# Feed-forward matmuls that read their moving columns as two interleaved halves

## The chip, the cores and the metric

The kernel runs on one core of a Trainium2 chip. The metric is device time in microseconds (us), the median of several runs of the same program.

## What is computed

Eight sequences of 3008 tokens with 256 features go through a spectral layer (a real Fourier transform along the sequence, a complex 256x256 product with a bias, a soft threshold, the inverse transform) and then, token by token, through a feed-forward layer:

```python
def _moe_ref(x, w_in, w_out):
    h = x @ w_in              # 24064 x 256 by 256 x 2048
    g = h * np.cos(h)
    return (g @ w_out).astype(np.float32)   # 2048 x 256
```

## The kernel before

**The spectral layer** is done by stages of small matmuls that the program calls `stage_a`, `stage_b` and `stage_c` (with special versions for the first sequences). The last of them, `stage_c`, leaves the tokens of a sequence with the features on the partitions, as a pair of float32r tiles `xTh` and `xTl` (a high part and the rest), for a tile of 512 tokens at a time: two chunks `c` of 128 features, each with 512 tokens side by side (lines 723 to 725). A sequence has six such tiles, five of 512 tokens and a last one of 448.

**The feed-forward layer** runs over sequences `b`, token tiles `t` and 16 chunks `f` of 128 hidden features. A step (`moe_step`, lines 765 to 790) has six matmuls into a PSUM tile `ph`, with the weights as the stationary operand and the tokens as the moving one: for each of the two feature chunks the high weights by `xTh` (line 772), the high weights by `xTl` (line 773) and the low weights by `xTh` (line 774). The cosine follows on ScalarE and VectorE (lines 779 to 783), then a split of the result into `gh` (ScalarE, line 784) and `gl` (VectorE or GpSimd, lines 785, 148 and 151). Three steps later (`SKEW`) `second` takes the pair up, with six more matmuls into two PSUM tiles `po`, the moving operand being `gh` (lines 742 and 743) and `gl` (line 748; line 745 in the very last step):

```python
mm(h, win[:, 0, c, fs], th[:, c, :n], start=c == 0, stop=False)
...
mm(po[e][:, :n], wo[0][:, 0, f, es], gh[:, :n], start=f == first, stop=False)
```

Here `n` is 512 or 448, and each of these operands is a run of `n` consecutive float32r words on each of 128 partitions. That is 8 x 6 x 16 = 768 steps of 12 matmuls, 9216 in all.

**The order.** While one sequence is in the feed-forward layer, the spectral stages of the next two are woven between its steps: `pull` in `moe_step` takes pieces of them by a budget of written costs (lines 866 to 875), so the order on TensorE is fixed when the program is built. The first stages, before the first feed-forward step, are written out by hand.

**Other matmuls that the prediction uses.** Line 323 multiplies plain float32 tiles of 96x512 (not float32r), line 520 plain float32 tiles of 128x256. **Other reads that it uses.** Line 299 copies a PSUM tile `p` of 128x512 to SBUF in another order, in turn on ScalarE and VectorE:

```python
(nc.vector.tensor_copy if n % 2 else nc.scalar.copy)(
    dst[:, :, :, 2 * n:2 * n + 2], p.rearrange("p (j c m) -> p c m j", j=2, c=2)[:, :, :96])
```

With `j` innermost it reads word 0, word 256, word 1, word 257 and so on. Line 201 reads every second word of an SBUF tile. Lines 724, 762, 783 and 784 read runs of consecutive words.

**The host** puts the result's columns, which come out by tile, back in the order of the sequence (line 919).

Of the kernel before, what the change touches and what calls it, by code (L numbers as in the profile page):

```python
# [19 lines left out]
NB, N, D, FF = 8, 3008, 256, 2048  # L20
# [7 lines left out]
NTT = 6  # L28
# [29 lines left out]
def _index():  # L58
    n1, n2 = np.arange(64), np.arange(48)
    return (47 * n1[:, None] + 64 * n2[None, :]) % N  # L60


def _constants():
# [50 lines left out]
def tile_body(ctx: ExitStack, tc, x, x2, w_r, w_i, b_r, b_i, w_in, w_out,  # L114
# [27 lines left out]
    win = cp.tile([128, 2, 2, FF], F32R, name="win")  # L142
    wo = [cp.tile([128, 2, NFC, 256], F32R, name="wout")]

    mm = nc.tensor.matmul
# [87 lines left out]
    raws, mark = [], {}  # L233
# [493 lines left out]
            yield 0.49  # L727


    pend = []  # L730
    outs, part = {}, {}

    def second(b, t, f, gh, gl):
        n = 512 if t < NTT - 1 else 448
        first, last_f = next((lo, hi - 1) for v, lo, hi in phases(b) if v == t and lo <= f < hi)
        if f == first:
            outs[0] = [ps.tile([128, 512], F32, tag=f"o{e}", name=f"po{e}", bufs=1) for e in range(2)]
        po = outs[0]
        end = (b, t, f) == (NB - 1, NTT - 1, NFC - 1)
        for e in range(2):  # L740
            es = slice(128 * e, 128 * e + 128)
            mm(po[e][:, :n], wo[0][:, 0, f, es], gh[:, :n], start=f == first, stop=False)  # L742
            mm(po[e][:, :n], wo[0][:, 1, f, es], gh[:, :n], start=False, stop=False)  # L743
            if end:
                mm(po[e][:, :n], wo[0][:, 0, f, es], gl[:, :n], start=False, stop=True)
        for e in range(0 if end else 2):
            es = slice(128 * e, 128 * e + 128)
            mm(po[e][:, :n], wo[0][:, 0, f, es], gl[:, :n], start=False, stop=f == last_f)  # L748
        if f != last_f:
            return  # L750
        for e in range(2):
            if last_f < NFC - 1:
                part[t, e] = wk.tile([128, 512], F32, tag=("yh", "yl", "z")[t], name="part", bufs=2)
                nc.scalar.copy(part[t, e], po[e])  # L754
                continue
            if e == 0:
                outs[1] = pool["mo"].tile([128, 2, 512], F32, tag="ob", name="ob", bufs=1)
            ob = outs[1][:, e]
            if first:
                nc.vector.tensor_tensor(out=ob, in0=po[e], in1=part.pop((t, e)), op=ALU.add)  # L760
            else:
                (nc.vector.tensor_copy if end and e else nc.scalar.copy)(ob[:, :n], po[e][:, :n])
            nc.sync.dma_start(out[b, e, :, 512 * t:512 * t + n], ob[:, :n])

    def moe_step(b, t, f, pull):
        th, tl = xT[b, t]
        n = 512 if t < NTT - 1 else 448
        ph = ps.tile([128, 512], F32, tag="h", name="ph", bufs=3)
        h = ph[:, :n]
        fs = slice(128 * f, 128 * f + 128)  # L770
        for c in range(2):
            mm(h, win[:, 0, c, fs], th[:, c, :n], start=c == 0, stop=False)  # L772
            mm(h, win[:, 0, c, fs], tl[:, c, :n], start=False, stop=False)  # L773
            mark["ph"] = mm(h, win[:, 1, c, fs], th[:, c, :n], start=False, stop=c == 1)  # L774
        u = pool["mo"].tile([128, 512], F32, tag="u", name="u", bufs=4)
        k = u.bitcast(I32)
        gh = pool["mo"].tile([128, 512], F32R, tag="gh", name="gh", bufs=SKEW + 1)
        gl = pool["mo"].tile([128, 512], F32R, tag="gl", name="gl", bufs=SKEW + 1)
        nc.scalar.activation(k[:, :n], h, AF.Identity, bias=0.25, scale=1.0 / TWO_PI)  # L779
        nc.vector.scalar_tensor_tensor(out=u[:, :n], in0=h, scalar=1.0 / TWO_PI, in1=k[:, :n],  # L780
                                       op0=ALU.mult, op1=ALU.subtract)
        nc.scalar.activation(u[:, :n], u[:, :n], AF.Sin, bias=HALF_PI, scale=TWO_PI)  # L782
        nc.vector.tensor_tensor(out=u[:, :n], in0=h, in1=u[:, :n], op=ALU.mult)  # L783
        mark["gh"] = nc.scalar.copy(gh[:, :n], u[:, :n])  # L784
        (rest_pool if b == 0 and t < 3 and f < 8 or f % 4 in POOL_GL else rest)(gl[:, :n], u[:, :n], gh[:, :n])
        pend.append((b, t, f, gh, gl))
        pull()
        if len(pend) > SKEW:
            second(*pend.pop(0))
        pull()  # L790
# [3 lines left out]
    with tc.manual_schedule(), ExitStack() as first:  # L794
# [4 lines left out]
        p = ps.tile([128, 512], F32, tag="o0", name="pz", bufs=1)  # L799
# [17 lines left out]
    def phases(b):  # L817
        if b == 0:
            return [(t, f, f + 8) for f in (0, 8) for t in range(3)] + [(t, 0, NFC) for t in range(3, NTT)]
        return [(t, 0, NFC) for t in range(NTT)]  # L820
# [38 lines left out]
    for b in range(NB):  # L859
        fa = ahead(b)  # L860
        for i, (t, lo, hi) in enumerate(phases(b)):
            budget = [0.0]
            open_ = [True]
            cost = share(b, i) + C_COST * (len(c_next(b, i)) if i < len(phases(b)) - 1 else 1)
            hold = C_FROM if b == i == 0 else 0
            rate = cost / (hi - lo - 1 - hold) / 2

            def pull():
                budget[0] += rate
                while open_[0] and budget[0] > 0:  # L870
                    c = next(fa, None)
                    if c is None:
                        open_[0] = False
                    else:
                        budget[0] -= c

            for f in range(lo, hi):
                if b == 0 and i < FIRST_B:
                    if i or f >= W_FROM:
                        due += W_RATE  # L880
                    while due >= 1.0:
                        due -= 1.0
                        next(mw, None)
                moe_step(b, t, f, pull if f >= hold else lambda: None)
            while open_[0]:
                c = next(fa, None)
                if c is None:
                    open_[0] = False
            if hi == NFC:
                del xT[b, t]  # L890
    for p in pend:
        second(*p)
# [28 lines left out]
```

## Time and profile before

| what | us |
|---|---|
| median of 3 runs | 2629.59 (2629.4 to 2632.5) |
| the profiled execution, its own time | 2629.45 |
| its span, from the first to the last instruction | 2627.7 |

In the rows further down, PE is TensorE's matmuls, PEld its weight loads, DVE VectorE, ACT ScalarE, POOL GpSimd; L742 is line 742. A row of a group gives the line, the engine, the operation, the names of what is written and read with their shapes and a count, then the busy time of the group, the mean duration of one in ns, and idle time ahead of it. Matmuls overlap, and the profile models their ends, so the mean of one is not what it costs in a row of many: for that the difference of two starts is read from the timeline.

### The profile page before, as it was taken

The numbers are of one execution on the slowest core, as the hardware profiler recorded it, in microseconds if no ns is written. First come the engines' busy times: TensorE is split into PE (matmuls) and PEld (weight loads), VectorE is DVE, ScalarE is ACT, GpSimd is POOL, SyncE is SP. The second block draws the span as 40 slices with busy tenths as digits, with TensorE's granted clock in tenths as the row PEclk, the third lists the DMA queues.
The fourth block names the chain that finished last, engine by engine and source line by source line (L and its number), as shares of the span: only waits on it lengthen the run. The fifth ranks groups of instructions, "written<-read, shape, count | busy, mean of one in ns | idle before, by whom it ended". The sixth has DMA issues, their size and how long they took to land.

```text
span 2627.7 us, 38433 instructions
## 1 busy us (share of the span) xinstructions
PE 2618.9 (100%) x13180; PEld 2241.8 (85%) x13180; DVE 1917.8 (73%) x3237; ACT 1877.2 (71%) x3557; POOL 1085.3 (41%) x916
## 2 busy tenths in 40 slices
PE   9999999999999999999999999999999999999999
PEld 8788888888888888888888888888888888888888
DVE  6888876877667776777767777677776666766665
ACT  5787766777677776777767777677776666666666
POOL 5774543544334443344423444244442333322222
PEclk9999999999999999999999999999999999999999
DMA  7533312322123222233212232123221111010000
GB/s 208 177 97 98 105 61 77 94 87 90 55 60 93 86 85 59 60 93 98 75 56 62 91 96 75 55 62 103 89 71 53 47 53 43 25 54 22 9 17 16
DMA packets 126373, 194.26 MB, mean 74 GB/s; under 512 B 14131, under 2 KB 63619, under 8 KB 126177
## 3 DMA queue, kind: packets, MB, share of 16 engines
q1 hardware_dynamic: 120160, 171.94, 21.5%
q0 software_dynamic: 6016, 19.86, 2.4%
q8 instruction: 104, 1.70, 0.3%
q14 instruction: 93, 0.75, 0.1%
HBM read 119.92 MB, written 71.83 MB: 73 GB/s over the span
## 4 chain that ended last, share of the span: by engine, by line
PE 99%; DMA 0%; DVE 0%; SPq 0%; issue 0%; ACT 0%; ACTq 0%
PE ph L772 13%; PE po L742 13%; PE po L743 13%; PE ph L773 13%; PE po L748 13%; PE ph L774 13%; PE pc L715 4%; PE pb L396 3%; PE p L422 2%; PE p L421 2%; PE p L420 2%; PE pi L460 2%; PE pa L364 2%; PE p L520 1%; PE pa L323 1%; PE pa L297 0%
## 5 line engine op out<-in xcount | busy, mean ns | idle before, releaser
L148 POOL TENSOR_TENSOR gl<-u,gh 128x512 fp32r<-128x512 f32 (+1 forms) x396 | 507.8, 1283 | 958.0 <-ACT gh L784 754.9
L783 DVE TENSOR_TENSOR u<-ph,u 128x512 f32<-128x512 f32 (+1 forms) x768 | 520.5, 678 | 275.6 <-ACT u L782 258.5
L780 DVE SCALAR_TENSOR_TENSOR u<-ph,u 128x512 f32<-128x512 f32 (+1 forms) x768 | 518.9, 676 | 252.0 <-ACT u L779 242.4
L779 ACT ACTIVATE u<-ph 128x512 int32<-128x512 f32 (+1 forms) x768 | 450.1, 587 | 253.0 <-PE ph L774 241.2
L782 ACT ACTIVATE u<-u 128x512 f32<-128x512 f32 (+1 forms) x768 | 479.5, 625 | 202.1 <-DVE u L780 199.1
L772 PE MATMUL ph<-xTh,win 128*128 128x512 f32 (+1 forms) x1536 | 611.5, 398 | 1.4 <-DVE u L783 1.1
L742 PE MATMUL po<-gh,wout 128*128 128x512 f32 (+1 forms) x1536 | 598.7, 390 | 0.0
L774 PE MATMUL ph<-xTh,win 128*128 128x512 f32 (+1 forms) x1536 | 595.1, 387 | 0.0
L773 PE MATMUL ph<-xTl,win 128*128 128x512 f32 (+1 forms) x1536 | 595.1, 387 | 0.0
L743 PE MATMUL po<-gh,wout 128*128 128x512 f32 (+1 forms) x1536 | 594.8, 387 | 0.0
L784 ACT CAST gh<-u 128x512 fp32r<-128x512 f32 (+1 forms) x768 | 467.2, 609 | 137.1 <-DVE u L783 134.9
L748 PE MATMUL po<-gl,wout 128*128 128x512 f32 (+1 forms) x1534 | 477.0, 388 | 0.0
L774 PEld LDWEIGHTS ph<-xTh,win 128*128 128x128 f32 x1536 | 288.8, 188 | 54.4
L742 PEld LDWEIGHTS po<-gh,wout 128*128 128x128 f32 x1536 | 289.0, 188 | 51.7 <-ACT part L754 0.3
L743 PEld LDWEIGHTS po<-gh,wout 128*128 128x128 f32 x1536 | 289.0, 188 | 51.6
L772 PEld LDWEIGHTS ph<-xTh,win 128*128 128x128 f32 x1536 | 289.1, 188 | 49.6 <-DVE u L783 2.0
L748 PEld LDWEIGHTS po<-gl,wout 128*128 128x128 f32 x1534 | 285.6, 188 | 51.9
L773 PEld LDWEIGHTS ph<-xTl,win 128*128 128x128 f32 x1536 | 289.5, 188 | 46.0
L151 DVE TENSOR_TENSOR gl<-u,gh 128x512 fp32r<-128x512 f32 (+1 forms) x372 | 274.2, 737 | 49.8 <-ACT gh L784 42.2
L148 POOL TENSOR_TENSOR xh<-xt,xh 48x512 fp32r<-48x512 f32 x144 | 188.5, 1310 | 205.9 <-ACT xh L352 179.4
L446 POOL TENSOR_TENSOR z<-z,cl 128x512 f32<-128x512 f32 x84 | 110.0, 1309 | 208.4 <-DVE cl L445 197.6
L367 DVE TENSOR_TENSOR ao<-pa,ao 48x512 f32<-48x512 f32 x192 | 133.0, 693 | 22.2 <-ACT ao L366 17.1
(122 smaller groups left out, 3108.1 us busy)
## 6 DMA issues: line engine op xcount, KB each, us to landing
xt<-in_dram SPq DMA_DIRECT2D x192, 224.0 KB, 2.7
scr<-bo SPq DMA_DIRECT2D x95, 256.0 KB, 2.0
bt<-scr SPq DMA_DIRECT2D x96, 240.0 KB, 3.2
at<-scr SPq DMA_DIRECT2D x84, 256.0 KB, 2.7
out_dram<-ob SPq DMA_DIRECT2D x80, 256.0 KB, 2.2
scr<-ao SPq DMA_DIRECT2D x192, 96.0 KB, 1.9
fb<-in_dram POOLq DMA_DIRECT2D x46, 256.0 KB, 3.3
raw<-in_dram POOLq DMA_DIRECT2D x14, 512.0 KB, 4.3
```

Source lines behind the costliest of these rows:

```text
L148: return nc.gpsimd.tensor_tensor(out=lo, in0=x, in1=hi.bitcast(F32), op=ALU.subtract)
L742: mm(po[e][:, :n], wo[0][:, 0, f, es], gh[:, :n], start=f == first, stop=False)
L743: mm(po[e][:, :n], wo[0][:, 1, f, es], gh[:, :n], start=False, stop=False)
L748: mm(po[e][:, :n], wo[0][:, 0, f, es], gl[:, :n], start=False, stop=f == last_f)
L772: mm(h, win[:, 0, c, fs], th[:, c, :n], start=c == 0, stop=False)
L773: mm(h, win[:, 0, c, fs], tl[:, c, :n], start=False, stop=False)
L774: mark["ph"] = mm(h, win[:, 1, c, fs], th[:, c, :n], start=False, stop=c == 1)
L779: nc.scalar.activation(k[:, :n], h, AF.Identity, bias=0.25, scale=1.0 / TWO_PI)
L780: nc.vector.scalar_tensor_tensor(out=u[:, :n], in0=h, scalar=1.0 / TWO_PI, in1=k[:, :n], op0=ALU.mult, op1=ALU.subtract)
L782: nc.scalar.activation(u[:, :n], u[:, :n], AF.Sin, bias=HALF_PI, scale=TWO_PI)
L783: nc.vector.tensor_tensor(out=u[:, :n], in0=h, in1=u[:, :n], op=ALU.mult)
L784: mark["gh"] = nc.scalar.copy(gh[:, :n], u[:, :n])
```

## The change

All 9216 feed-forward matmuls take their moving operand through a new helper, `woven`, which orders the `n` columns as column 0, column n/2, column 1, column n/2 + 1 and so on; in words of the partition, 0, 256, 1, 257 for `n` = 512, and 0, 224, 1, 225 for 448. The stationary operand and the output are as before: the results are written side by side, in the order in which the columns are read. So `ph` holds the tokens in an order that is woven once, `po` in one that is woven twice, and the host undoes it with `_order`. No instruction is added or taken away, and no engine but TensorE is given another operand.

```diff
+def _order():
+    at = []
+    for t in range(NTT):
+        n = min(512, N - 512 * t)
+        w = np.arange(n).reshape(2, n // 2).T.reshape(-1)
+        at.append(512 * t + w[w])
+    return np.concatenate(at)
...
+    def woven(v):
+        return v.rearrange("p (b a) -> p a b", b=2)
+
...
-            mm(po[e][:, :n], wo[0][:, 0, f, es], gh[:, :n], start=f == first, stop=False)
-            mm(po[e][:, :n], wo[0][:, 1, f, es], gh[:, :n], start=False, stop=False)
+            mm(po[e][:, :n], wo[0][:, 0, f, es], woven(gh[:, :n]), start=f == first, stop=False)
+            mm(po[e][:, :n], wo[0][:, 1, f, es], woven(gh[:, :n]), start=False, stop=False)
...
-            mm(po[e][:, :n], wo[0][:, 0, f, es], gl[:, :n], start=False, stop=f == last_f)
+            mm(po[e][:, :n], wo[0][:, 0, f, es], woven(gl[:, :n]), start=False, stop=f == last_f)
...
-            mm(h, win[:, 0, c, fs], th[:, c, :n], start=c == 0, stop=False)
-            mm(h, win[:, 0, c, fs], tl[:, c, :n], start=False, stop=False)
-            mark["ph"] = mm(h, win[:, 1, c, fs], th[:, c, :n], start=False, stop=c == 1)
+            mm(h, win[:, 0, c, fs], woven(th[:, c, :n]), start=c == 0, stop=False)
+            mm(h, win[:, 0, c, fs], woven(tl[:, c, :n]), start=False, stop=False)
+            mark["ph"] = mm(h, win[:, 1, c, fs], woven(th[:, c, :n]), start=False, stop=c == 1)
...
-    res[:, idx[:, :47].reshape(2, 32, 47).transpose(1, 0, 2).reshape(-1)] = got
+    res[:, idx[:, :47].reshape(2, 32, 47).transpose(1, 0, 2).reshape(-1)[_order()]] = got
```

## Rows read from the trace of the kernel before

**Rows 1.** Page: busy us of each engine, then granted TensorE clock in 40 slices.
```profile
PE 2618.9 (100%) x13180; PEld 2241.8 (85%) x13180; DVE 1917.8 (73%) x3237; ACT 1877.2 (71%) x3557; POOL 1085.3 (41%) x916
...
PEclk9999999999999999999999999999999999999999
```
**Rows 2.** Page: the chain that ended last, shares by engine and by line.
```profile
PE 99%; DMA 0%; DVE 0%; SPq 0%; issue 0%; ACT 0%; ACTq 0%
PE ph L772 13%; PE po L742 13%; PE po L743 13%; PE ph L773 13%; PE po L748 13%; PE ph L774 13%; PE pc L715 4%; PE pb L396 3%; PE p L422 2%; PE p L421 2%; PE p L420 2%; PE pi L460 2%; PE pa L364 2%; PE p L520 1%; PE pa L323 1%; PE pa L297 0%
```
**Rows 3.** Groups by shape on PE: some of the feed-forward lines.
```profile
L772 PE MATMUL ph<-xTh,win 128*128 128x512 f32 x1280 | 513.4, 402 | 1.4 <-DVE u L783 1.1 <-ACT xTh L724 0.3
...
L742 PE MATMUL po<-gh,wout 128*128 128x512 f32 x1280 | 504.4, 394 | 0.0
...
L742 PE MATMUL po<-gh,wout 128*128 128x448 f32 x256 | 94.3, 368 | 0.0
...
L748 PE MATMUL po<-gl,wout 128*128 128x448 f32 x254 | 73.0, 367 | 0.0
...
L745 PE MATMUL po<-gl,wout 128*128 128x448 f32 x2 | 0.6, 366 | 0.0
```
**Rows 4.** Timeline, a step of 512 columns: start us, us, engine, line.
```profile
2559.85 0.39 PE L742 MATMUL po<-gh,wout 128*128 128x512 f32 x1
...
2560.08 0.19 PEld L742 LDWEIGHTS po<-gh,wout 128*128 128x128 f32 x1
...
2562.57 0.39 PE L742 MATMUL po<-gh,wout 128*128 128x512 f32 x1
```
**Rows 5.** Timeline, the last tile, of 448 columns.
```profile
2617.82 0.36 PE L772 MATMUL ph<-xTh,win 128*128 128x448 f32 x1
...
2622.08 0.36 PE L742 MATMUL po<-gh,wout 128*128 128x448 f32 x1
```
**Rows 6.** Timeline, plain float32 matmuls of 512 and of 256 columns.
```profile
87.58 3.60 PE L323 MATMUL pa<-xq,fa 96*96 96x512 f32 x8
91.01 1.88 PE L323 MATMUL pa<-xt,fa 96*96 96x512 f32 x4
...
27.76 1.03 PE L520 MATMUL p<-wi,Xf 128*128 128x256 f32 x4
```
**Rows 7.** Groups by shape on PE: the same plain float32 lines.
```profile
L520 PE MATMUL p<-wi,Xf 128*128 128x256 f32 x48 | 12.3, 380 | 0.0
...
L323 PE MATMUL pa<-xq,fa 96*96 96x512 f32 x8 | 3.6, 592 | 0.0
```
**Rows 8.** Groups by shape on ACT: interleaved, consecutive and second-word reads.
```profile
L784 ACT CAST gh<-u 128x512 fp32r<-128x512 f32 x640 | 395.1, 618 | 111.9 <-DVE u L783 109.7
...
L784 ACT CAST gh<-u 128x448 fp32r<-128x448 f32 x128 | 72.1, 564 | 25.2 <-DVE u L783 25.2
...
L201 ACT ACTIVATE wm<-raw 128x512 f32<-128x512 f32 x16 | 10.9, 679 | 0.0
...
L299 ACT COPY a<-pa 128x384 f32<-128x384 f32 x8 | 3.9, 490 | 13.8 <-PE pa L297 13.8
L724 ACT CAST xTh<-pc 128x376 fp32r<-128x376 f32 x8 | 3.8, 473 | 0.9 <-PE pc L715 0.9
L724 ACT CAST xTh<-pc 128x386 fp32r<-128x386 f32 x8 | 3.8, 470 | 0.3 <-DVE xTl L725 0.3
```
**Rows 9.** Groups by shape on DVE: consecutive and interleaved reads.
```profile
L783 DVE TENSOR_TENSOR u<-ph,u 128x512 f32<-128x512 f32 x640 | 440.6, 689 | 219.9 <-ACT u L782 206.8
...
L783 DVE TENSOR_TENSOR u<-ph,u 128x448 f32<-128x448 f32 x128 | 79.9, 624 | 55.7 <-ACT u L782 51.7
...
L299 DVE COPY a<-pa 128x384 f32<-128x384 f32 x8 | 4.5, 558 | 15.1 <-PE pa L297 15.1
...
L762 DVE COPY ob<-po 128x448 f32<-128x448 f32 x1 | 0.6, 625 | 1.1 <-PE po L745 1.1
```

More of the change, by code (lines that the diff above doesn't have):

```diff
@@ L741, in second @@
             es = slice(128 * e, 128 * e + 128)
-            mm(po[e][:, :n], wo[0][:, 0, f, es], gh[:, :n], start=f == first, stop=False)
-            mm(po[e][:, :n], wo[0][:, 1, f, es], gh[:, :n], start=False, stop=False)
+            mm(po[e][:, :n], wo[0][:, 0, f, es], woven(gh[:, :n]), start=f == first, stop=False)
+            mm(po[e][:, :n], wo[0][:, 1, f, es], woven(gh[:, :n]), start=False, stop=False)
             if end:
-                mm(po[e][:, :n], wo[0][:, 0, f, es], gl[:, :n], start=False, stop=True)
+                mm(po[e][:, :n], wo[0][:, 0, f, es], woven(gl[:, :n]), start=False, stop=True)
         for e in range(0 if end else 2):
             es = slice(128 * e, 128 * e + 128)
-            mm(po[e][:, :n], wo[0][:, 0, f, es], gl[:, :n], start=False, stop=f == last_f)
+            mm(po[e][:, :n], wo[0][:, 0, f, es], woven(gl[:, :n]), start=False, stop=f == last_f)
         if f != last_f:
```

## The prediction

> **What bounds the kernel now.** First the page's busy times [rows 1]: TensorE has matmuls under way in 2618.9 us of a span of 2627.7, and nothing else comes near it. A busy TensorE need not be a full one, so the chain of waits is read next [rows 2]: 99% of what ended last is TensorE, and 13% each are the six lines of the feed-forward layer, 78% together. Hardly anything makes TensorE wait: the dearest idle time ahead of a feed-forward line is 1.4 us in the whole run [rows 3]. So the end is set by how fast TensorE takes one matmul after the other, and whatever a feed-forward matmul gains or loses reaches the end in full. [...]
>
> **What one costs** is read from the timeline, as the difference of starts, since the listed durations overlap. From one L742 to the L742 twelve matmuls later it is 2562.57 - 2559.85 = 2.72 us [rows 4], 0.2267 us for one of 512 columns: 213.3 ns for the columns at a cycle each, and 13.4 ns over. In the last tile 21 matmuls of 448 columns take 2622.08 - 2617.82 = 4.26 us [rows 5], 0.2029 us each: 186.7 ns and 16.2 over. The weight load ahead of each lasts 0.19 us [rows 4] and fits beside the matmul before. The counts [rows 3]: 1280 of 512 columns on each of six lines, 7680; and 256 of 448 on each (254 and 2 for the last line), 1536. Check: 7680 x 0.2267 + 1536 x 0.2029 = 1740.8 + 311.6 = 2052.4 us, 78% of the span, as the chain says. In columns: 7680 x 512 + 1536 x 448 = 4.620 million.
>
> **The change, part by part.** It removes, adds and moves no instruction, no DMA and no wait; the order on the queues of SP, POOL and the others stays that of the written budgets. The output of each matmul is still written side by side, so lines 779 to 785 and the copies of `po` read what they read before, in another order of tokens. The host's reordering is no device time. The weight loads read the same words. All that cost nothing, and no cover is needed for it. One thing is left: the moving operand's address jumps by 256 (or 224) words at each column, instead of going up by one. Its price is that of 4.620 million columns, times what a column gets dearer.
>
> **That price is not in the trace.** No TensorE instruction here reads its moving columns other than in order. It is bounded from both sides:
>
> - Below: nothing. A gain is all but excluded: the columns already come at a cycle each, and were the 13.4 and 16.2 ns over them to vanish, it would be 7680 x 0.0134 + 1536 x 0.0162 = 128 us, a time of 2502; I see no way in which jumps of address could do that.
> - The rows with this very order of words are line 299's, in PSUM and not in SBUF. On DVE 384 words take 558 ns; consecutive ones take 625 for 448, and at 65 ns for 64 words (689 less 624) that is 560 for 384: no price [rows 9]. On ACT they take 490 ns, consecutive 376 and 386 take 473 and 470: 18 ns or 0.047 ns a word [rows 8]. Line 201 (every second word, in SBUF) takes 679 where line 784 takes 618, another function: at most 61 ns for 512 words, 0.12 ns a word [rows 8]. But these engines want a word in 1.02 ns (DVE, 65 / 64) or in 0.84 ns (ACT, 54 / 64, from 618 and 564); TensorE wants one in 0.4167. They prove that jumping reads come at about 0.84 ns a word, and say nothing of twice that pace.
> - Above: the slowest pace so proved, DVE's 1.02 ns a column. That is 0.60 ns more than now, 4.620 million x 0.60 = 2770 us, a time of about 5400.
>
> **The value I take is half the present pace**, 0.833 ns a column, two cycles. It is the pace nearest to TensorE for which rows vouch: ACT's 0.84 ns for jumping words [rows 8], and TensorE's own pace wherever it does not stream at full speed. The plain float32 matmuls of line 323 take (3.60 - 0.592) / 7 = 0.4297 us for 512 columns (four of them: 1.288 / 3 = 0.4293), those of line 520 (1.03 - 0.380) / 3 = 0.2167 us for 256 [rows 6, 7]: 0.832 ns a column. Full pace then needs two words for each such step, and a word that lies 1,024 bytes from the last cannot come with it. That last sentence is an inference of mine, from paces alone.
>
> [...]
>
> The sum for half pace, against the profiled execution's own 2629.45 us (0.14 below the median of the runs, so no correction): 7680 x 0.2133 + 1536 x 0.1867 = 1638.4 + 286.7 = 1925 us more, **4554 us**. That keeps the 13 to 16 ns over the columns. Its ends: with line 323's 0.4297 in their place, and 0.4297 - 64 x 0.000832 = 0.3765 for 448 columns, it is 7680 x 0.2030 + 1536 x 0.1736 = 1826 us more, 4455; with everything doubled, what lies over the columns too, 2052 more, 4682. I take the middle one, since the rows have no reason for the overhead to go or to grow. What hides beside TensorE has more room than before: DVE's 1917.8 us and ACT's 1877.2 [rows 1] would be 42% and 41% of such a span. [...]
>
> **The rivals.**
>
> - *No change* (2629). [...] For it: line 299's copies, whose order is the same and which pay nothing on DVE and 4% on ACT; each 16 bytes are still used in full, every other access. Against it: they stand at 0.84 to 1.02 ns a word. The point that decides is whether alternating reads can be fed at 0.4167 ns. That the change does not do what it says belongs here too: if the access pattern were put back in rising order when the program is built, the time would be this one; the output's flat order makes that improbable. 0.16 together.
> - *A small loss*: ACT's 0.047 ns a word on line 299, 4.620 million x 0.047 = 217 us, 2846 us. For it: that row. Against it: it has to hold at more than twice ACT's pace. 0.04.
> - *Every second jump costs a cycle*, as when one of two accesses finds its line ready: 4.620 million x 0.208 = 963 us, 3592 us. No row for it; it is the middle between two cases. 0.06.
> - *Dearer than half pace*: the jump costs its latency each time, up to DVE's pace as above, to 5400 us. Against it: ACT's 0.84 ns with jumps. 0.10.
> - *Faster*, the 13 to 16 ns gone, 2502 us: 0.02.
>
> **How the numbers follow.** Half pace has the rest, 0.62, and its own range is 4455 to 4682. The predicted time is its, 4554. The range has to reach to other cases to leave out no more than 2 in 10: going down it takes in the middle, the small loss and no change, 0.88 together, from 2625 (0.2% below now) to 4690; what stays out is the dearer case and the gain. Going up instead, to 5400, would be wider and hold less. A measurement of this kernel tells about 0.2% from no change: faster 0.02, within it 0.16, slower 0.82.
>
> **What the profile after would show.** Right: the same twelve matmuls from L742 to L742 take about 5.28 us (0.440 each) and not 2.72; the mean of a feed-forward matmul rises from 394 ns to about 600, as line 323's 592; lines 323 and 520 keep their pace; the granted clock is full; TensorE is still busy all along and DVE and ACT drop to some 42%. Wrong: 2.72 us again (the read path keeps up); or 3.5 to 4.2 us, or above 5.6, with the clock full (the price of a jump is another); or TensorE idle before a feed-forward line, with ACT or DVE named as what it waited for; or a lower granted clock, which would put a part of the loss on the clock and not on the read.

## The result, and the profile after

The median went from 2629.49 to **2516.89 us**: a ratio of 0.957, with a 95% interval of 0.9554 to 0.9587. That is 113 us faster, where 1925 us slower was forecast. The measured time lies outside the range, on the side that had a chance of 0.02.

The page after: busy times, granted clock, and the chain's shares by engine.

```profile
PE 2502.2 (99%) x13180; PEld 2251.6 (90%) x13180; DVE 1914.6 (76%) x3237; ACT 1861.2 (74%) x3557; POOL 1075.8 (43%) x916
...
PEclk9999999999999999999999999999999999999999
...
PE 91%; DVE 5%; ACT 2%; issue 1%; DMA 1%; SPq 0%; POOL 0%; ACTq 0%; DVEq 0%; POOLq 0%
```

Beside [rows 1] and [rows 2]: the counts are the same, the clock is as full as before, and TensorE's busy time fell by 116.7 us. Its idle time in the span went from 8.8 (2627.7 - 2618.9) to 12.7 us (2514.9 - 2502.2), which gives 3.9 of it back: 112.8 us, the fall of the span. So the whole result is matmuls that follow one another faster.

The timeline after, for the stretch of 512 columns and the last tile of 448 (the lines stand 12 lower in the file than before: L754 was L742, L784 was L772):

```profile
2446.10 0.38 PE L754 MATMUL po<-gh,wout 128*128 128x512 f32 x1
...
2448.69 0.38 PE L754 MATMUL po<-gh,wout 128*128 128x512 f32 x1
...
2505.94 0.35 PE L754 MATMUL po<-gh,wout 128*128 128x448 f32 x1
...
2508.21 0.35 PE L754 MATMUL po<-gh,wout 128*128 128x448 f32 x1
```

Twelve matmuls take 2.59 us for 2.72 in [rows 4], 0.2158 each. With 448 columns twelve take 2.27 us, 0.1892 each, where [rows 5] gave 0.2029. From 448 to 512 columns the pitch (start to start) now rises by 26.7 ns, 0.4167 ns a column, the figure that the prediction counts for a column. Over 512 and 448 columns at that pace, 213.3 and 186.7 ns, stand 2.5 ns each, where it was 13.4 and 16.2. With 0.4167 ns counted for each column, before and after, what went is the time on top: 7680 x 0.0109 + 1536 x 0.0137 = 105 us of the 113. The rest is that in order not every matmul had the pitch of this stretch. From all starts in the two traces, a feed-forward matmul of 512 columns that another one follows took 231.9 ns on the mean before, with a median of 227 and over a quarter of them at 231 or more, and 219.1 after, with a median of 216. In all, the time from a feed-forward matmul to the next start fell by 119.4 us, and that of the other matmuls rose by 6.7. The groups, whose means are of overlapping durations, say the same:

```profile
L784 PE MATMUL ph<-xTh,win 128*128 128x512 f32 x1280 | 497.6, 389 | 2.1 <-DVE u L795 1.8 <-ACT xTh L733 0.3
...
L754 PE MATMUL po<-gh,wout 128*128 128x512 f32 x1280 | 488.8, 382 | 1.5 <-ACT part L766 1.4
...
L754 PE MATMUL po<-gh,wout 128*128 128x448 f32 x256 | 90.9, 355 | 0.0
```

Against [rows 3] the means fell from 402 to 389, from 394 to 382 and from 368 to 355 ns, 12 to 13 each.

### The profile page after: what moved, and what is told of

Its sections match the earlier page's. It is cut to its first block, busy times and chain, and to the rows that moved or that the text cites. A ratio compares the mean times of both kernels' runs of the same rounds, so it can differ in the third digit from the quotient of the medians.

```text
span 2514.9 us, 38433 instructions
## 1 busy us (share of the span) xinstructions
PE 2502.2 (99%) x13180; PEld 2251.6 (90%) x13180; DVE 1914.6 (76%) x3237; ACT 1861.2 (74%) x3557; POOL 1075.8 (43%) x916
## 4 chain that ended last, share of the span: by engine, by line
PE 91%; DVE 5%; ACT 2%; issue 1%; DMA 1%; SPq 0%; POOL 0%; ACTq 0%; DVEq 0%; POOLq 0%
PE po L754 12%; PE po L755 12%; PE ph L784 12%; PE po L760 12%; PE ph L786 12%; PE ph L785 12%; PE pc L724 4%; PE pb L405 3%; PE p L429 2%; PE p L430 2%; PE p L431 2%; PE pi L469 2%; PE pa L373 2%; PE p L529 1%; DVE u L795 1%
## 5 line engine op out<-in xcount | busy, mean ns | idle before, releaser
L157 POOL TENSOR_TENSOR gl<-u,gh 128x512 fp32r<-128x512 f32 (+1 forms) x396 | 501.8, 1268 | 886.0 <-ACT gh L796 462.9
L784 PE MATMUL ph<-xTh,win 128*128 128x512 f32 (+1 forms) x1536 | 592.0, 386 | 2.1 <-DVE u L795 1.8
L754 PE MATMUL po<-gh,wout 128*128 128x512 f32 (+1 forms) x1536 | 579.7, 377 | 1.5 <-ACT part L766 1.4
L786 PE MATMUL ph<-xTh,win 128*128 128x512 f32 (+1 forms) x1536 | 576.6, 375 | 0.0
L755 PE MATMUL po<-gh,wout 128*128 128x512 f32 (+1 forms) x1536 | 575.9, 375 | 0.0
L785 PE MATMUL ph<-xTl,win 128*128 128x512 f32 (+1 forms) x1536 | 575.5, 375 | 0.0
L760 PE MATMUL po<-gl,wout 128*128 128x512 f32 (+1 forms) x1534 | 458.0, 376 | 0.0
L754 PEld LDWEIGHTS po<-gh,wout 128*128 128x128 f32 x1536 | 290.4, 189 | 34.4 <-ACT part L766 1.8
L784 PEld LDWEIGHTS ph<-xTh,win 128*128 128x128 f32 x1536 | 290.2, 189 | 33.2 <-DVE u L795 2.9
```

What stands on the lines that cost most here:

```text
L157: return nc.gpsimd.tensor_tensor(out=lo, in0=x, in1=hi.bitcast(F32), op=ALU.subtract)
L754: mm(po[e][:, :n], wo[0][:, 0, f, es], woven(gh[:, :n]), start=f == first, stop=False)
L755: mm(po[e][:, :n], wo[0][:, 1, f, es], woven(gh[:, :n]), start=False, stop=False)
L760: mm(po[e][:, :n], wo[0][:, 0, f, es], woven(gl[:, :n]), start=False, stop=f == last_f)
L784: mm(h, win[:, 0, c, fs], woven(th[:, c, :n]), start=c == 0, stop=False)
L785: mm(h, win[:, 0, c, fs], woven(tl[:, c, :n]), start=False, stop=False)
```

## The experiments

Four questions stood in a row: is it the weight load, the neighbours or the read itself; is it one layer alone; which orders pay and which cost; and why.

### Rows of matmuls alone

A kernel without the computation: rows of 36 matmuls, one row per line of code, on one pair of tiles, most of them of float32r. The comments in the excerpts of these kernels are added; `il(v, b)` reads `v` as `b` interleaved parts.

```diff
+seg(lambda i, p, s: mm(p[:, :512], wt[:, :128], mv[:, :512], **s))          # in order
+seg(lambda i, p, s: mm(p[:, :512], wt[:, :128], il(mv[:, :512], 2), **s))   # two parts, as the change
+seg(lambda i, p, s: mm(p[:32], wt[:, :32], mv[:, :512], **s))               # 32 stationary columns
...
```

> Not the kernel: it leaves the whole computation out and runs rows of 36 matmuls each, alone on the chip, all on the same two tiles; one thing differs from row to row (columns, order of the moving columns, columns of the stationary operand, type). The pitch (start to start) is read for each row. Theory A, the excess over a cycle a column (13 ns at 512 columns) is the reads of the next weight load that get in the way of the moving stream, and interleaving lets it dodge: in order 0.227 and interleaved 0.216 us at 512 columns, and the excess in order falls to about 8 ns with 64 and to about 5 ns with 32 stationary columns. Theory B, it is the moving read by itself, words in order being the dearer ones whatever is loaded beside it: 0.227 and 0.216 us, and the same excess with 64 and 32 stationary columns. Theory C, the excess is contention with the other engines and DMA queues that share SBUF: with nothing else running both orders take 0.216 us.

The chain in order of time: start, us of the row, line, count. One matmul's pitch is the us over the count.

```profile
17.20 8.16 PE p L51 x36
25.36 7.77 PE p L52 x36
33.13 7.30 PE p L53 x36
40.43 6.81 PE p L54 x36
...
91.72 8.34 PE p L63 x36
100.06 7.77 PE p L64 x36
107.83 10.19 PE p L65 x36
118.01 17.61 PE p L66 x36
135.62 15.60 PE p L67 x36
...
166.75 16.24 PE p L69 x36
182.99 11.81 PE p L70 x36
194.80 9.00 PE p L71 x36
...
270.40 7.79 PE p L80 x36
278.19 17.44 PE p L81 x36
295.62 30.90 PE p L82 x72
326.52 38.88 PE p L83 x72
...
373.59 8.52 PE p L85 x36
```

The weight loads of two of these rows (groups by shape on PEld):

```profile
L51 PEld LDWEIGHTS p<-mv,wt 128*128 128x128 f32 x36 | 6.8, 188 | 1.4
...
L63 PEld LDWEIGHTS p<-mv,wt 128*32 128x32 f32 x36 | 3.9, 109 | 4.4
```

L51 and L52 are 512 columns in order and in two parts: 0.2267 and 0.2158 us, the two pitches of the kernel. Nothing else ran, so **theory C falls**. L53 and L54 are 448 columns: 0.2028 and 0.1892, again the kernel's. L63 and L64 have 32 stationary columns: 0.2317 and 0.2158. The weight load is shorter (109 ns for 188) and the excess no smaller, so **theory A falls** and B stands: it is the moving read by itself.

The rows after them were the surprise. Four parts (L65) take 0.283 us, eight (L66) 0.489, sixteen (L67) 0.433, and 256 parts, which is every second word and then the others (L69), 0.451. So interleaving in two gains, interleaving in more costs time, and from eight parts on it costs about what was forecast for two, or more. L80 and L81 are bfloat16: 0.2164 in order, and 0.484 in two parts. L82 and L83 are plain float32, where each matmul stands as two in the trace: 0.429 in order, 0.540 in two parts. **Of the three types, two parts pay for float32r alone.** L70 and L71 take blocks of two and of four words in turn from the two halves (0, 1, 256, 257, 2, 3 and so on for L70): 0.328 and 0.250 us. L85 reads 512 columns in order from the second word on: 0.2367. These three come up again under "Why".

### One layer alone

```diff
-            mm(po[e][:, :n], wo[0][:, 0, f, es], woven(gh[:, :n]), start=f == first, stop=False)
+            mm(po[e][:, :n], wo[0][:, 0, f, es], gh[:, :n], start=f == first, stop=False)
...
-        at.append(512 * t + w[w])
+        at.append(512 * t + w)
```

> Only the six matmuls into ph read interleaved; those into po read in order (the host's order is once woven). A and B: half of the gain, the pitch of the ph lines 0.216 and of the po lines 0.227 us, a time of about 2573 us. C: the gain could sit in one layer alone, since gh and gl are written by ScalarE, VectorE and GpSimd just before they are read and the tokens are not: then this one is near 2630 or near 2517.

> Only the matmuls into po read interleaved; those into ph read in order. A and B: half of the gain, about 2573 us, po lines at 0.216 and ph lines at 0.227 us. C: the rest of what the run with the first layer alone did not gain.

With the first layer alone it took 2575.42 us (in brackets the ratio to the kernel before, with its 95% interval: 0.979, 0.9774 to 0.9807), and with the second alone 2576.22 (0.9794, 0.9779 to 0.9808): half of the gain each. The gain sits where the edit does: by the starts in the traces, with 512 columns, the lines that read interleaved have a median of 216 ns in both runs, those left in order 227 to 232. Operands written just before they are read gain as much as tokens written long before.

### Sixteen parts in the kernel

```diff
...
-        return v.rearrange("p (b a) -> p a b", b=2)
+        return v.rearrange("p (b a) -> p a b", b=16)
```

> The same change with 16 interleaved parts in place of 2 (columns 0, 32, 64 and so on; the host's order goes with it). The first rows of matmuls alone showed 0.433 us for 512 columns in 16 parts. If a row alone tells what the kernel pays: 7680 x (0.433 - 0.227) + 1536 x (0.379 - 0.203) = 1852 us more than before, about 4480 us. If the neighbours in the kernel hide or add to it, something else. That is the price that the prediction had set for two parts.

One run took 4533.16 us. Timeline, 512 columns and then the last tile of 448:

```profile
2563.01 0.61 PE L784 MATMUL ph<-xTh,win 128*128 128x512 f32 x1
...
2564.74 0.62 PE L755 MATMUL po<-gh,wout 128*128 128x512 f32 x1
...
4519.72 0.61 PE L754 MATMUL po<-gh,wout 128*128 128x448 f32 x1
...
4524.68 0.61 PE L754 MATMUL po<-gh,wout 128*128 128x448 f32 x1
```

Four of 512 columns take 1.73 us, 0.4325 each, as alone. Twelve of 448 take 4.96, 0.4133 each and not the 0.379 that was scaled down: 1536 x 0.034 = 53 us, as much as the time stood above the 4480 expected. With 512 columns the price in a row alone is the price in the kernel (sixteen parts of 448 columns were not run alone). A pace of about half exists, for another order than the one that was to be forecast.

### Which orders pay

```diff
+seg(lambda i, p, s: mm(p, wt[:, :128], loc(mv[:, :512], 4), **s))   # within 4 words: 0 2 1 3, 4 6 5 7
+seg(lambda i, p, s: mm(p, wt[:, :128], loc(mv[:, :512], 8), **s))   # within 8 words: 0 4 1 5 2 6 3 7
+seg(lambda i, p, s: mm(p, wt[:, :128], far(257), **s))              # 0 257 1 258 and so on
...
```

> Not the kernel: it leaves the whole computation out and runs rows of 36 matmuls each, as the first such run, with other orders of the moving columns. Theory B1: TensorE takes float32r columns in two streams, the first, third, fifth and so on by one and the second, fourth and so on by the other, each with a line of its own, and what costs is that in order both want the same lines. Then interleaving within 8 words (0, 4, 1, 5, 2, 6, 3, 7, 8, 12 and so on) already takes 0.216 us for 512 columns, as do 16, 32, 64 and 128, while within 4 words (0, 2, 1, 3) it stays at 0.227 us or above. Theory B2: it is the distance, two far places of memory being served side by side and near ones not: within 8 and 16 words it takes 0.227 us or more, and only wide ones reach 0.216; then the price should also move with the distance between the halves (257 to 512 words). Theory B3: it is a price paid at the start of a matmul, the same for any number of columns: 480, 416, 352 and 320 columns in order all lie 11 to 14 ns over the interleaved ones, and a row that alternates the two orders lies in the middle, at 0.221 us. A price by line read would instead fall from 11 ns at 512 columns to 7 at 320.

```profile
33.47 8.19 PE p L59 x36
41.66 7.77 PE p L60 x36
...
80.51 7.77 PE p L65 x36
...
150.46 7.82 PE p L74 x36
158.28 7.29 PE p L75 x36
...
189.85 5.28 PE p L80 x36
195.12 4.89 PE p L81 x36
...
216.59 8.37 PE p L84 x36
224.96 8.16 PE p L85 x36
...
313.37 8.23 PE p L94 x36
...
329.38 9.76 PE p L96 x36
```

Within 4 words (L59) 0.2275 us, within 8 (L60) 0.2158, and the same 0.2158 within 16, 32, 64 and 128. The line of the expectations is a group of four words, 16 bytes, counted from a multiple of four. That it has four words shows in 0.2275 us within 4 against 0.2158 within 8; where it counts from shows in the order within 8 begun two words and one word further on, 0.2278 and 0.2667 us (L88 and L89 under "Why"). Halves that are 257 words apart (L65), 260, 264 and up to 512 are all at 0.2158 (258 at 0.2164). So **B2 falls**: between two halves, distance plays no part. B3 falls in one half: the row that alternates the two orders (L94) takes 0.2286 and not the mean, 0.2213. The other half is not settled: in order costs 14.7 ns more than interleaved with 480 columns (L74, L75) and 10.8 with 320 (L80, L81), near the 11 to 14 of B3, but this is a fall by 27% where the columns fall by 33%. L84 and L85 are 512 columns in order from word 32 and from word 64 on, 0.2325 and 0.2267 us, and L96 is bfloat16, two words in turn from each half, 0.271; they are used further down.

### Near orders in the kernel

```diff
...
-        return v.rearrange("p (b a) -> p a b", b=2)
+        return v.rearrange("p (n b a) -> p n a b", b=2, a=4)
```

With `a=2` in its place it is the order within 4 words.

> The change with another order: interleaved within each 8 words (columns 0, 4, 1, 5, 2, 6, 3, 7, 8, 12 and so on), so that no column is read further than 4 words from its neighbour; the host's order goes with it. Theory B1 (two streams, dear where both want the same 16-byte line): neighbours in time always lie on different lines and each stream reads its line to the end, so all of the gain stays, about 2517 us. Theory B2 (the halves have to be far apart): no gain, about 2630 us.

> The change with the order interleaved within each 4 words (columns 0, 2, 1, 3, 4, 6, 5, 7 and so on): as many jumps, but both streams stay on one line. Theory B1: the gain is gone, alone such a row took 0.2275 us for 512 columns against 0.2267 in order, so 2630 to 2637 us. If it were the jumping as such that helps, or an access pattern of more than one dimension, about 2517 us.

Within 8 words: 2514.28 us (0.956, 0.9546 to 0.9574), all of the gain (the change has 0.957, 0.9554 to 0.9587). Within 4 words: 2629.7 (0.9999, 0.999 to 1.0009), no change at all, though as many columns jump. So jumping as such neither helps nor hurts; it depends on which words lie at every second place.

### Why

B1 had two things in one: the streams share a line in order, and each finds only two of its words on it.

```diff
+seg(lambda i, p, s: mm(p, wt[:, :128], mv[:, :256].unsqueeze(2).to_broadcast([128, 256, 2]), **s))   # 0 0 1 1 2 2
+seg(lambda i, p, s: mm(p, wt[:, :128], part(2), **s))                                                 # 0 4 1 5, 8 12 9 13
...
```

> Not the kernel: it leaves the whole computation out and runs rows of 36 matmuls each, as the two runs of that kind before. What is open is what makes the order side by side dear: that both streams stand on the same line at the same time, or that each finds only two of its words on a line before it needs the next. A row that reads only the first two words of each line in the order 0, 4, 1, 5, 8, 12, 9, 13 and so on has two words per line and stream and never a shared line: 0.216 us for 512 columns if the shared line is what costs, 0.227 or more if it is the two words. A row that reads each word twice (0, 0, 1, 1 and so on) has four per line and stream, on a line that is always shared: 0.227 us or more if the sharing costs, 0.216 if it is the number of words. With 480 columns, interleaving within 6, 10, 12, 20, 24 words, where a line is at times shared and at times not, lies between 0.2172 (in order) and 0.2025 us by either. The excess in order at other numbers of columns, 440 to 504, shows whether it grows with them: it should rise by 0.2 ns for each 8 columns more if it is paid by line, and not at all if by matmul.

```profile
17.74 8.16 PE p L57 x36
25.90 7.77 PE p L58 x36
33.67 7.77 PE p L59 x36
...
49.21 8.28 PE p L61 x36
57.49 16.24 PE p L62 x36
...
88.83 7.80 PE p L65 x36
96.63 9.12 PE p L66 x36
105.75 7.29 PE p L67 x36
113.05 8.39 PE p L68 x36
121.44 7.29 PE p L69 x36
...
263.05 8.20 PE p L88 x36
271.25 9.60 PE p L89 x36
```

Each word twice (L59) takes 0.2158 us although by B1 both streams are always on one line, and two words per line and stream without a shared line (L61) take 0.2300. So a shared line is neither enough for the price (L59, which however goes to a new line half as often) nor needed for it (L61). With that, **B1's reason, the shared line, falls, and the number of words stays**. Taking every second column as a stream by itself, and lines of four words: four in a row on a line cost nothing (0.2158); two in a row cost some 11 to 14 ns a matmul (in order, L57, 0.2267; L61, 0.2300); one costs double (L62, the first two words of each line in order, 0.4511). The rows of 480 columns fit: within 4 words (L65) 0.2167 as in order, within 8 (L67) 0.2025; within 6 (L66) and 10 (L68), which cut lines so that single words are left over, 0.2533 and 0.2331, dearer than in order, where the expectation had them in between. So does the order within 8 words when it starts two words (L88, 0.2278) or one word (L89, 0.2667) off a line: there too words are left over. That four words, counted from a multiple of four, make the group is what these rows and the two runs of the kernel above show.

That TensorE has two such streams for float32r is a reading; no run shows it directly, and these rows do not fit it:

- Within 12 words (L69, 480 columns) each stream finds four words and two words in turn, and yet nothing is paid: 0.2025 us.
- Blocks of two and of four words in turn from two halves (L70 and L71 of the first rows) give each stream one and two words at a time, but took 0.328 and 0.250 us, where the reading has 0.451 and 0.227 to 0.230. Four parts, one word at a time as well, took 0.283.
- In order the price moves with the place of the first word. From 1, 4, 8, 16 and 32 words further on, 512 columns took 0.2367, 0.2317, 0.2336, 0.2289 and 0.2325 us, from 64, 128 and 256 again 0.2267; yet a start at 4, 8, 16 or 32 leaves every word at the same place of its line. In two parts a start at 1 or 8 took 0.2167 and 0.2158. This may be why over a quarter of these matmuls in the kernel before took 231 ns or more; no run tells.

What stays open with it is the form of the price at two words. From 256 to 480 columns it is 8.3 to 14.7 ns, about 0.03 ns a column; but it is 10.9 with 512, and from 440 to 504 it lies between 13 and 20 in no order. So shown is which orders are cheap and which are dear, and that the words at every second place decide; the mechanism behind it is open.

### The other float32r matmuls

```diff
...
-                    mm(p, xh[:, comp, c], wf[:, j, 0, c], start=first and c == 0, stop=False, skip_group_check=True)
+                    mm(p, xh[:, comp, c], woven(wf[:, j, 0, c]), start=first and c == 0, stop=False, skip_group_check=True)
...
-            mm(p, fas, ld.pop(i), start=True, stop=True)
+            mm(p, fas, woven(ld.pop(i)), start=True, stop=True)
...
```

> All of the change, and two kinds of the other float32r matmuls read interleaved as well: the 1512 of 256 columns (lines 429 to 431), whose weights are stored the other way round so that what comes out is in the old order, and the 192 of line 373, whose input the host lays out accordingly. Theory B, any float32r stream in order pays: 256 columns alone took 0.1200 in order and 0.1117 us interleaved, so 1512 x 0.0083 + 192 x 0.011 = 14.7 us less than after, about 2502 us. If the gain is one of the feed-forward lines alone, no difference from 2517.

2505.94 us (0.9529, 0.9516 to 0.9542), 11 us less than after, where 14.7 were expected. TensorE's busy time fell by 13.0, from 2502.2 to 2489.2 us, and its idle time rose from 12.7 to 15.0.

```diff
-            nc.scalar.copy(yh, z)
-            rest_pool(yl, z, yh)
+            nc.scalar.copy(yhv, zv)
+            rest_pool(ylv, zv, yhv)
...
```

> As the run before, and the inverse transform's 231 matmuls of 512 and 42 of 256 columns (line 469) too; here ScalarE and GpSimd write their operand the other way round. Theory B: 231 x 0.011 + 42 x 0.008 = 2.9 us less than the run before, about 2499 us, if the jumping writes of ScalarE and GpSimd cost little; were each of the 84 writes on GpSimd twice as long (1.3 us more), the chain through it could take the gain back.

2519.99 us (0.9583, 0.957 to 0.9596), 14 us more than the run before. Groups on ACT and POOL of this run, and the chain's first line:

```profile
L461 ACT CAST yh<-z 128x512 fp32r<-128x512 f32 x84 | 94.4, 1124 | 6.6 <-POOL z L456 4.9
...
L157 POOL TENSOR_TENSOR yl<-z,yh 128x512 fp32r<-128x512 f32 x84 | 121.6, 1447 | 77.8 <-ACT yh L461 74.7 <-PE ph L790 1.5 <-PE pb L406 1.4
...
PE 72%; DVE 12%; ACT 9%; issue 4%; DMA 2%; POOL 1%; ACTq 0%; SPq 0%; DVEq 0%; POOLq 0%
```

ScalarE's copy took 1124 ns where it had taken 618, GpSimd's subtraction 1447 where it had taken 1297. The warning in the expectation came true, though mostly on another engine: ScalarE's jumping write took 506 ns more, GpSimd's 150. The two were changed together, so what each costs at the end is not shown. TensorE's share of the chain fell from 89 to 72%.

```diff
-            nc.scalar.copy(bo, p)
+            nc.scalar.copy(bo.rearrange("p (k b a) -> p k b a", k=2, b=2),
+                           p.rearrange("p (k a b) -> p k b a", k=2, b=2))
```

> As the run with the Fourier products and line 373 interleaved, and the inverse transform's matmuls too, but with no jumping write: yh and yl are written side by side, line 470 reads them interleaved within each 256, and ScalarE's copy of the result (bo) reads PSUM at every second word to put the order right. 231 x 0.011 + 42 x 0.008 = 2.9 us less than 2506, so 2503 us, if that copy costs ScalarE as little more as the interleaved copy of PSUM before the change (4%); if PSUM read at every second word were as dear as the jumping writes to SBUF were (619 to 1124 ns), slower than 2506.

2503.7 us (0.9521, 0.9507 to 0.9535); its runs, 2501.96 to 2506.2, overlap those at 2505.94, so the last 2 us are not shown. The copy that reads every second word of PSUM took 577 ns, as the plain one did (578). This run and the first of this section are the fastest versions: faster than the change by 11 to 13 us.

## Why the prediction was wrong

**Right:** what bounds the kernel. TensorE's start to start set the end, a gain there reached the end nearly in full, no other engine or queue set the time (the chain after has 91% TensorE for 99), and the clock stayed full. Right too that nothing but the moving read changes.

**The step that failed** is "The value I take is half the present pace", with the inference under it, that full pace needs two words for each step and that "a word that lies 1,024 bytes from the last cannot come with it". In its place: with two parts 512 columns took 0.2158 us, 0.4167 ns a column (0.2133) and 2.5 ns. The paces from which it was drawn, those of plain float32 and of ScalarE, did not carry over to float32r. The price exists in sixteen parts, 4533 us, inside the 4455 to 4682 given for two; but that a word on a far line cannot come in time is not its reason, since two parts, the order within 8 words and halves up to 512 words apart all go to another line at each column and took 0.2158. One row under the step was also misread: [rows 6] and [rows 7] count passes, not matmuls. Line 323 runs 16 times and has 8 and 24 records, as the 36 matmuls of L82 have 72, so a plain float32 matmul of 512 columns takes two passes of 0.43 us. The pace in a pass, which the prediction used, is as it says. The sum itself counts 213.3 and 186.7 ns for the columns, "at a cycle each". No run shows a cycle or its length; what the runs show in its place is that in orders that pay the pitch rises by 0.4167 ns a column (36 matmuls of 512 columns took 7.77 us, L60 of the second rows, and of 320 columns 4.89 us, L81).

**The second failure** is the bound below, "A gain is all but excluded", and with it the 0.02. The size of that case was nearly right: 13.4 and 16.2 ns over the columns, 128 us if all went; 10.9 and 13.7 of them went, 105 us by the pitch of these stretches and 113 in the median. What was missing is the question why they were there. [rows 6] held the hint: a plain float32 pass of the same length stands 0.4297 - 2 x 0.2133 = 3 ns over twice 0.4167 ns a column, so 13 to 16 ns need not be a fixed price of a matmul. It was used as an end of the range for half pace ("the rows have no reason for the overhead to go") and not as a sign that the read in order was itself slow.

**The rivals.** "No change" turned on whether alternating reads can be fed at 0.4167 ns a column. They could, 0.2158 us for 512; what it lacked is that reads in order were not (0.2267). The 16 bytes that it counts by, and the line of "Every second jump", are in the runs the group of four words (0.2275 us for the order within 4, 0.2158 within 8). "Every second jump" and "dearer" did not come; prices like theirs exist in other orders (0.328 us for the blocks of two words, where 0.2267 + 512 x 0.000208 = 0.333 would be the first; 0.489 for eight parts).

For bfloat16 the new orders were the dearer ones: 512 columns took 0.2164 us in order, 0.484 in two parts, and 0.271 with two words in turn from each half (L96 of the second rows).

## What to carry to other kernels

Where float32r matmuls bound a kernel, compare their start to start with what two parts took, 0.2158 us for 512 columns: 0.2267 leaves 11 ns to be had, by an order in which every second column walks along one group of four words, 16 bytes (0, 4, 1, 5, 2, 6, 3, 7 is enough), if the order can be undone for nothing, in the host's layout or in a PSUM copy (577 ns on ScalarE, for 578). With bfloat16, plain float32 or more than two parts the same edit cost time, up to 2.2 times as much (0.484 us for 0.2164). And an excess in a row is to be explained before it is called fixed: here it was the whole of the result.

## What was not expected of the hardware

- In order is not the fastest order for float32r: 0.2267 against 0.2158 us for 512 columns, with nothing else running.
- Every second word, in which each line is used twice, is a slow order for float32r (0.451 us), while a word of another line at each column can cost nothing more (0.2158).
- ScalarE's write to SBUF that jumps 128 words at each element took 1124 ns for 512 in place of 618; its read of every second word of PSUM took 577, for 578.
- For sixteen parts, 448 columns took 0.4133 us, nearly as long as 512 (0.4325). Columns that follow each other are 28 words apart in the one and 32 in the other, whole lines in both, so the place on a line does not explain it; the cause is open.
- In order the pitch depends on the first word: 0.2267 us from word 0 or 64, 0.2325 from word 32, 0.2367 from word 1.
